# Loading the exactness flag earlier, a branch without prefetch hints, and exps without a wait on their own engine

## The chip, the core and the metric

The kernel runs on one core of one Trainium2 chip. Each set of experiments was made on one chip, different sets on different chips. The metric is the device time of one execution in microseconds (us), as the median of several executions. PE is the matrix engine, ACT the scalar engine, DVE the vector engine, POOL the general one, SP the engine that only synchronises and starts transfers.

"The span" is the time that a profile of the core covers. The time is normally 1.8 us longer than the span (1.75 to 1.92 in the runs of the kernel before). SBUF and PSUM are the core's two on-chip memories.

## The reference

Layer norm of `x`, then multi-query attention (32 heads of 16, one shared key and value head) beside a SwiGLU block, whose result gates the attention's:

```python
xn = layernorm(x)                              # x: 1 x 2048 x 512, bf16
q  = (xn @ wq).reshape(B, S, 32, 16)           # one k and one v for all heads
p  = softmax(einsum("bhqd,bkd->bhqk", q, xn @ wk) * 16**-0.5)
s  = einsum("bhqk,bkd->bqhd", p, xn @ wv).reshape(B, S, 512) @ wo
g  = silu((silu(xn @ w_gate) * (xn @ w_up)) @ w_down)
return x + s * g
```

The kernel skips the softmax's subtraction of the row maximum. A check at the end tells whether the sums of the exponentials lay in a safe range; if not, a branch leads into a second, exact computation. With this data the check passes and the exact path never runs.

## The kernel before

Scores are made on PE, 1024 columns at a time, into PSUM (`ring`). ACT takes 772 such tiles through `exp` into one of eight SBUF buffers `Pb` (DVE does the others by arithmetic), and PE multiplies the result by the values. The host-side scheduler in the program fixes each engine's order; the framework adds the semaphore waits. An exp has two inputs to wait for: its scores, and the products on PE that read the older content of its buffer.

```python
NPB = 8
Pb = [sb([P, 1024], BF16, f"Pb{i}") for i in range(NPB)]
...
buf = Pb[k % NPB][:]
...
ex = OP("ACT", 0.904, [sc, pb_rel[k - NPB] if k >= NPB else None, cur["exp"]],
        lambda: nc.scalar.activation(out=buf, in_=ring[i][:], func=ACT.Exp, scale=escale, bias=ebias),
        (1,), name="exp")
```

The framework also sees that exp `k` overwrites what exp `k - 8` wrote, and gives it a wait on ACT itself. That makes two waits, and one of them needs an instruction of its own ahead of the exp. In the trace it is the wait on PE that stands in the extra instruction (733 times; twice it is one on DVE), while the exp itself carries the wait on ACT.

The end of the program: four last products on PE, four multiplications on DVE, four additions on POOL and DVE, four stores from SP. The flag is loaded into a register of every engine, and every engine branches on it.

```python
tadd("DVE", e_out_mul(LN, obk[0], dsts[0]))
tadd("DVE", nc.vector.tensor_single_scalar(out=flag_i[:], in_=tq01[0:1, 0:1], scalar=P - 0.5, op=ALU.is_lt))
for en, et in (("SP", "SP"), ("POOL", "Pool"), ("PE", "PE"), ("DVE", "DVE"), ("ACT", "Activation")):
    with tc.issue_after(_last[en].ins):
        tc.mark_branch_hint_location("exact", "LikelyTaken", [getattr(mybir.EngineType, et)])
loads, vals = nc.values_load_multi_w_load_instructions(flag_i[0:1, 0:1])
flag = vals[0]
tadd("SP", [l for l in loads if l.ins.engine == nc.sync.engine])
fin_add(0, nc.gpsimd, "POOL")
tadd("DVE", e_out_mul(LN + 1, obk[1], dsts[1]))
tadd("DVE", e_out_mul(LN + 2, obk[2], dsts[2]))
fin_add(2, nc.gpsimd, "POOL")
fin_add(1, nc.vector, "DVE")
tadd("DVE", e_out_mul(LN + 3, obk[3], dsts[3]))
fin_add(3, nc.vector, "DVE")
for k in range(4):
    tadd("SP", e_out_st(LN + k))
MAIN.close()

with tc.If(flag > 0, label="exact"):
    _exact_max_path(...)                       # arguments cut
```

## Time and profile before

| | before |
|---|---|
| time, median of 3 | 781.65 us (780.74 to 781.86) |
| busy share of PE, ACT, DVE | 96%, 97%, 94% |
| last exp ends / last computing instruction ends / program ends | 766.1 / 774.1 / 780.2 us |
| extra wait instructions ahead of exps | 735 |

Three engines are almost always busy, so the shares don't tell which sets the pace. Three more views of this kernel are needed for what follows. First, the page's chain that ended last, by engine; "issue" is time in which the profile shows no cause for waiting:

```profile
PE 47%; ACT 37%; issue 8%; DVE 6%; POOL 0%; SPq 0%; DMA 0%; ACTq 0%; DVEq 0%; POOLq 0%
```

Second, ACT's timeline around two of its few real holes (start, length, what ran, the idle time before it and who ended it):

```profile
41.25 1.11 ACT L937 ACTIVATE Pb<-ring 128x1024 bf16<-128x1024 f32 x1
43.23 3.77 ACT L937 ACTIVATE Pb<-ring 128x1024 bf16<-128x1024 f32 x4 [0.86 <-PE ring L877]
...
462.71 1.16 ACT L937 ACTIVATE Pb<-ring 128x1024 bf16<-128x1024 f32 x1
464.29 2.85 ACT L937 ACTIVATE Pb<-ring 128x1024 bf16<-128x1024 f32 x3 [0.42 <-PE ring L877]
```

The engine stood idle for 0.86 and 0.42 us, and PE's scores ended that. In such a hole the nanoseconds between the scores and the exp can count.

Third, the 16 stores of the output from SP: duration of the issue (smallest, median, largest, in ns), and the time from issue to landing. Each store of 128 rows reports its landing in sixteen shares, and is done with the last:

```profile
L698 SPq DMA_DIRECT2D out_dram<-xn x16: 333/352/1392, 232.3 to 774.5; - x16
...
DMA to landing us min/median/max: 1.7/2.0/2.8
```

### The profile page before, as it was taken

How to read it: one execution, taken by the hardware profiler on the slowest of the kernel's cores; microseconds unless marked ns; L12 is line 12 of the kernel's file. 1: busy time of each engine (PE TensorE's matmuls, PEld its weight loads, DVE VectorE, ACT ScalarE, POOL GpSimd, SP SyncE). 2: the span in 40 equal slices, each digit the busy share in tenths (PEclk: the TensorE clock that was granted, in tenths of full speed). 3: DMA queues.
4: the chain of work that ended last, by engine and by line, in shares of the span. 5: the costliest groups of instructions: out<-in, count | busy, mean ns of one | idle time of the engine just before them, and what ended most of it. 6: DMA issues, size and time to landing. Idle time of an engine off the chain costs nothing.

```text
span 780.2 us, 21438 instructions
## 1 busy us (share of the span) xinstructions
PE 748.7 (96%) x9095; PEld 229.7 (29%) x9095; DVE 733.9 (94%) x920; ACT 757.1 (97%) x866; POOL 53.0 (7%) x59
## 2 busy tenths in 40 slices
PE   7999999999999999999999999999999999999994
PEld 3323223322222333322232322222223233322221
DVE  7689999999999999999999999999999999999994
ACT  6999999999999999999999999999999999999993
POOL 2100000000012000000001110000000300000001
PEclk9999999999999999999999999999999999999998
DMA  9400000000001000000000100000000000000001
GB/s 326 141 10 9 16 2 24 2 8 17 5 28 49 24 2 7 17 2 24 3 10 28 43 23 2 24 1 9 17 2 24 29 22 2 3 23 3 23 2 32
DMA packets 21199, 20.20 MB, mean 26 GB/s; under 512 B 8744, under 2 KB 17192, under 8 KB 21096
## 3 DMA queue, kind: packets, MB, share of 16 engines
q1 hardware_dynamic: 19512, 18.20, 7.7%
q8 instruction: 73, 1.20, 0.7%
q10 hardware_dynamic: 1584, 0.56, 0.3%
q14 instruction: 30, 0.25, 0.1%
HBM read 14.19 MB, written 2.34 MB: 21 GB/s over the span
## 4 chain that ended last, share of the span: by engine, by line
PE 47%; ACT 37%; issue 8%; DVE 6%; POOL 0%; SPq 0%; DMA 0%; ACTq 0%; DVEq 0%; POOLq 0%
ACT Pb L937 33%; PE ring L877 17%; PE m_ps L488 15%; PE o_ps L747 13%; ACT th L657 3%; DVE Bf L991 1%; ACT g_sb L937 1%; ACT th L674 1%; DVE Bf L1010 1%; DVE x_sb L1010 0%; PE ring L488 0%; DVE Bf L1005 0%; DVE Bf L1017 0%; DVE x_sb L991 0%; DVE x_sb L1005 0%
## 5 line engine op out<-in xcount | busy, mean ns | idle before, releaser
L937 ACT ACTIVATE Pb<-ring 128x1024 bf16<-128x1024 f32 x772 | 726.2, 1140 | 2.4 <-PE ring L877 2.3
L877 PE MATMUL ring<-QB,KT 32*128 32x512 bf16 x2048 | 306.1, 382 | 15.5 <-ACT Pb L937 9.1
L991 DVE TENSOR_SCALAR Bf<-ring 128x1024 uint16<-128x1024 f32 x172 | 209.7, 1219 | 5.5 <-PE ring L877 4.2
L877 PEld LDWEIGHTS <-KT 32*128 32x128 bf16 x2048 | 94.4, 91 | 314.2 <-issue 307.7
L747 PE MATMUL o_ps<-Pb,VA 128*32 128x512 bf16 x1544 | 146.9, 385 | 0.0
L991 DVE TENSOR_SCALAR x_sb<-ring 128x1024 uint16<-128x1024 f32 x72 | 87.8, 1219 | 3.1 <-PE ring L877 2.9
L1010 DVE TENSOR_TENSOR Bf<-Bf,Bf 128x2048 f16<-128x2048 f16 x74 | 90.1, 1217 | 0.1
L747 PE MATMUL o_ps<-xnT,zw 128*32 128x512 bf16 x1092 | 83.1, 381 | 0.0
L488 PE MATMUL m_ps<-xnT,wu_sb 128*32 128x512 bf16 x896 | 72.5, 384 | 1.1 <-DVE ab L659 1.1
L488 PE MATMUL m_ps<-wd_sb,hT 128*32 128x512 bf16 x896 | 71.5, 383 | 0.1
L488 PE MATMUL m_ps<-xnT,wg_sb 128*32 128x512 bf16 x896 | 70.3, 384 | 0.0
L747 PE MATMUL o_ps<-Bf,VD 128*32 128x512 f16 x688 | 67.1, 385 | 0.3 <-DVE Bf L1010 0.3
L732 POOL TENSOR_TENSOR oT<-oa,rb 128x512 bf16<-128x512 f32 x15 | 21.5, 1434 | 615.4 <-DMA rb<-dscr 365.9
L1017 DVE TENSOR_SCALAR Bf<-Bf 128x2048 uint16<-128x2048 uint16 x86 | 60.2, 700 | 0.6
L747 PEld LDWEIGHTS <-VA 128*32 128x32 bf16 x1560 | 37.9, 94 | 53.9 <-issue 51.5
L1005 DVE TENSOR_SCALAR Bf<-Bf 128x2048 uint16<-128x2048 uint16 x74 | 52.4, 716 | 0.0
L659 DVE SCALAR_TENSOR_TENSOR ab<-th,m_ps 128x512 f32<-128x512 f32 x56 | 38.1, 681 | 3.8 <-ACT th L657 3.4
L663 DVE TENSOR_TENSOR hT<-ab,m_ps 128x512 bf16<-128x512 f32 x56 | 38.2, 682 | 2.1 <-PE m_ps L488 1.7
L657 ACT ACTIVATE th<-m_ps 128x512 f32<-128x512 f32 x56 | 40.0, 714 | 0.0
L747 PEld LDWEIGHTS <-VD 128*32 128x32 f16 x976 | 26.4, 94 | 38.8 <-issue 35.2
L747 PEld LDWEIGHTS <-zw 128*32 128x32 bf16 x1092 | 25.8, 95 | 25.5 <-issue 12.9
L1010 DVE TENSOR_TENSOR x_sb<-x_sb 128x2048 f16<-128x2048 f16 x24 | 29.2, 1218 | 0.0
(121 smaller groups left out, 413.7 us busy)
## 6 DMA issues: line engine op xcount, KB each, us to landing
rb<-dscr SPq DMA_DIRECT2D x15, 256.0 KB
out_dram<-xn SPq DMA_DIRECT2D x16, 128.0 KB, 2.0
dn<-oa SPq DMA_DIRECT2D x120, 2.0 KB, 1.7
oa<-oa SPq DMA_DIRECT2D x60, 32.0 KB, 2.0
wg_sb<-in_B_w_gate_dram SPq DMA_DIRECT2D x1, 1792.0 KB, 11.5
wu_sb<-in_B_w_up_dram SPq DMA_DIRECT2D x1, 1792.0 KB
wd_sb<-in_B_w_down_dram SPq DMA_DIRECT2D x1, 1792.0 KB, 20.1
x_sb<-in_A_x_dram SPq DMA_DIRECT2D x3, 512.0 KB
```

Of the source, the lines that this page charges most:

```text
L488: return [nc.tensor.matmul(out=dst[GRP * j:GRP * j + GRP, :], lhsT=w[:, GRP * j:GRP * j + GRP], rhs=rhs, start=start, stop=stop, tile_posi ...
L657: t_ = OP("ACT", 0.477, [a], lambda: nc.scalar.activation(out=th[i][:], in_=m_ps[:], func=ACT.Tanh, scale=0.5), (0,), name="tanh")
L659: s_ = OP("DVE", 0.6, [t_, ab_rel[i]], lambda: nc.vector.scalar_tensor_tensor(out=ab[i][:], in0=th[i][:], scalar=1.0, in1=m_ps[:], op0=ALU ...
L663: h = OP("DVE", 0.6, [b], lambda: nc.vector.tensor_tensor(out=hT[:, f, :], in0=ab[i][:], in1=m_ps[:], op=ALU.mult), (1,), name="hmul")
L732: return [pk, q], lambda eng: eng.tensor_tensor(out=oT[qs % 2][:, jj, :], in0=o0[:], in1=rbt[:], op=ALU.mult)
L747: r.append(nc.tensor.matmul(out=o_ps[GRP * g:GRP * g + GRP, :], lhsT=lhs, rhs=rhs, start=(n == 0), stop=(n == pv_total[(b, g)] - 1), tile_ ...
L877: return lambda: [nc.tensor.matmul(out=ring[sl][:, u * 512:(u + 1) * 512], lhsT=KT[half][GRP * g:GRP * g + GRP, t * P:(t + 1) * P], rhs=QB ...
L937: lambda: nc.scalar.activation(out=buf, in_=ring[i][:], func=ACT.Exp, scale=escale, bias=ebias),
L991: lambda: nc.vector.tensor_scalar(out=U[:, hs], in0=ring[si][:], scalar1=ubias, scalar2=UINF, op0=ALU.add, op1=ALU.min), (1.5, u), name="p ...
L1005: o1 = OP("DVE", 0.6, [pa, pa0] + wrel, lambda: nc.vector.tensor_scalar(out=Bf[wi], in0=U, scalar1=0x3FF, scalar2=0x3800, op0=ALU.bitwise_and,
L1010: return lambda: eng.tensor_tensor(out=Bf[wi][:, a:z].bitcast(FP16), in0=Bf[wi][:, a:z].bitcast(FP16), in1=U[:, a:z].bitcast(FP16), op=ALU ...
L1017: o2 = OP("DVE", 0.6, o3, lambda: nc.vector.tensor_scalar(out=U, in0=U, scalar1=0x7C00, scalar2=None, op0=ALU.bitwise_and), (2, u, 1), nam ...
```

## The change

Its intent: take the self-waits off the exps, and with them 733 of the 735 extra instructions, let DVE have its flag early so that it can branch sooner, and drop the prefetch hints. The self-wait isn't needed: exp `k` waits for the products on PE that read exp `k - 8`'s output, and those waited for exp `k - 8`.

```diff
-    act_q = []
+    act_q, exp_ins = [], {}
...
-        ex = OP("ACT", 0.904, [sc, pb_rel[k - NPB] if k >= NPB else None, cur["exp"]],
-                lambda: nc.scalar.activation(out=buf, in_=ring[i][:], func=ACT.Exp, scale=escale, bias=ebias),
-                (1,), name="exp")
+        def emit():
+            bi = nc.scalar.activation(out=buf, in_=ring[i][:], func=ACT.Exp, scale=escale, bias=ebias)
+            if k >= NPB:
+                tc.declare_no_dep(bi.ins, exp_ins[k - NPB].ins,
+                                  reason="waits for the products on PE that read the older exp's output")
+            if k >= 0:
+                exp_ins[k] = bi
+            return bi
+        ex = OP("ACT", 0.904, [sc, pb_rel[k - NPB] if k >= NPB else None, cur["exp"]], emit, (1,), name="exp")
...
-    for en, et in (("SP", "SP"), ("POOL", "Pool"), ("PE", "PE"), ("DVE", "DVE"), ("ACT", "Activation")):
-        with tc.issue_after(_last[en].ins):
-            tc.mark_branch_hint_location("exact", "LikelyTaken", [getattr(mybir.EngineType, et)])
...
     fin_add(2, nc.gpsimd, "POOL")
+    tadd("DVE", [l for l in loads if l.ins.engine == nc.vector.engine])
     fin_add(1, nc.vector, "DVE")
...
-    with tc.If(flag > 0, label="exact"):
+    with tc.If(flag > 0):
```

The flag itself is computed at the same place in both kernels. Only its load on DVE moves.

## The prediction

> **What bounds the kernel now.** I began with the page. The span is 780.2 us (781.65 us is the timed median), and three engines are busy for nearly all of it, so shares alone don't name the bound:
>
> ```profile
> PE 748.7 (96%) x9095; PEld 229.7 (29%) x9095; DVE 733.9 (94%) x920; ACT 757.1 (97%) x866; POOL 53.0 (7%) x59
> ...
> L937 ACT ACTIVATE Pb<-ring 128x1024 bf16<-128x1024 f32 x772 | 726.2, 1140 | 2.4 <-PE ring L877 2.3
> ```
>
> The second line is the group of exps that the third part of the change edits. The reader should see that ACT sat idle for only 2.4 us before 772 exps. Next I read the instructions of that line: 735 exps have one extra instruction of the sequencer, a semaphore wait of 17 ns, because they wait on two things, PE (scores) and ACT itself (the older exp that wrote the same buffer).
>
> ```profile
> L937 ACT ACTIVATE Pb<-ring x772: 1017/1135/1317, 12.9 to 764.9; 128x1024 bf16<-128x1024 f32 x193
> L937 ACTq EVENT_SEMAPHORE  x735: 17/17/17, 12.1 to 764.7; - x184
> ```
>
> Then the timeline of ACT in mid-kernel: four overlapping narrow windows, each giving a merged pair (start, length from the first's start to the second's end), and one wide window.
>
> ```profile
> 504.20 2.07 ACT L937 ACTIVATE Pb<-ring 128x1024 bf16<-128x1024 f32 x2
> 505.10 2.08 ACT L937 ACTIVATE Pb<-ring 128x1024 bf16<-128x1024 f32 x2
> 506.00 2.09 ACT L937 ACTIVATE Pb<-ring 128x1024 bf16<-128x1024 f32 x2
> 506.97 2.04 ACT L937 ACTIVATE Pb<-ring 128x1024 bf16<-128x1024 f32 x2
> 501.47 11.21 ACT L937 ACTIVATE Pb<-ring 128x1024 bf16<-128x1024 f32 x12
> ```
>
> Starts are 0.90, 0.90 and then 0.97 us apart, as if the last exp had been late by 0.06. But the ends (start plus length) are 506.27, 507.18, 508.09, 509.01: 0.91 to 0.92 apart, with no hole. The wide window says the same: the first exp of the twelve took 1.13 us by its own record, so (11.21 - 1.13) / 11 = 0.916 us from end to end. From the trace's single records, 687 of the 697 directly consecutive pairs have an end-to-end step below 0.93 us, almost all 0.915 to 0.918. The engine delivers an exp every 0.917 us, whatever the starts do: ACT is the bound from about 14 us to 766 us, and only a hole between ends is lost time.
>
> Last, the end of the program. The last computing instruction ends at 774.07 us; the last 6.2 us are stores, branches and the closing waits, read from the instructions of the flag load (L1358) and the branch (L1372):
>
> ```profile
> L1358 SPq TENSOR_LOAD <-flag_i x1: 474/474/474, 770.7 to 770.7; - x1
> L1358 DVEq TENSOR_LOAD <-flag_i x1: 543/543/543, 773.2 to 773.2; - x1
> ...
> L1372 SPq EVENT_SEMAPHORE  x8: 17/17/17, 777.9 to 778.8; - x8
> ...
> L1372 PEldq COMPARE_BRANCH  x1: 3705/3705/3705, 771.3 to 771.3; - x1
> ...
> L1372 DVEq COMPARE_BRANCH  x1: 84/84/84, 773.8 to 773.8; - x1
> ...
> L1372 SPq COMPARE_BRANCH  x1: 70/70/70, 775.3 to 775.3; - x1
> ...
> L1372 DVEq EVENT_SEMAPHORE  x1: 21/21/21, 776.9 to 776.9; - x1
> ```
>
> SP is last. Its branch is at 775.35, after the four stores, and its next instruction, the first of 16 waits on landings, runs at 777.85. The semaphore of the fourth store gets its sixteenth landing at 778.37 (fifteen were in by 776.99), and the waits and the barrier after it take to 780.23. So the tail ends by the last share of the last store; SP's own branch, done at 777.85, is 0.52 us behind that as second limit. DVE is back at 776.94 and has 1.4 us to spare.
>
> **What the Trainium skill says.** "Perfetto Trace Analysis", section "DVE / Act Engine Instruction", puts an event-wait queue and an execution FIFO between sequencer and engine: while one ACTIVATE executes, the next is decoded and waits there. The trace agrees: the extra wait usually passes some 0.1 to 0.6 us ahead of its exp's start, while the previous exp still runs. The same page, "Identifying Dependency Chains", says that an instruction with waits on several engines may have semaphore instructions put ahead of it; those are the 735. "Runtime: NRT & Kernel Launch", section "Instruction fetch mechanics", says that a taken branch whose target isn't loaded forces a fetch by DMA before execution goes on. The trace agrees: after their branches ACT, DVE and SP stand still for 2.5, 3.1 and 2.4 us, PE's branch itself takes 3.7, and fetches of 8 or 16 KB appear 0.6 to 1.1 us after each; it also shows no fetch within 2 us after any of the five prefetch hints, so they seem to have bought nothing here.
>
> **The change, part by part.** The order of instructions was compared engine by engine. The flag is computed at the same place as before; only the five hints go, DVE's load of the flag moves up ahead of the last two adds and one product, and exps waiting on both PE and ACT fall from 733 to 0 of 780 (2 with a wait on DVE stay). Nothing else moves.
>
> 1. *Self-waits.* Where an exp's scores come late, the trace gives the price: from PE's semaphore update to the exp's start it is 83 ns by way of the extra wait, and 23 ns for activations that wait on PE directly. So 60 ns per exp whose lateness is felt. Felt means a hole between ends. The list of end-to-end steps over 0.93 us has 11 entries, 3.4 us together beyond 0.917 (0.58 of it at the very start). Eight of them end with an exp released 83 ns before through the extra wait. One is only 0.02 us deep, seven can give back the whole 60 ns: 7 x 0.06 + 0.02 = 0.44 us. The other hundred or so exps that start late leave no hole: 0. The 17 ns themselves lie beside a running exp: 735 x 0. **Sum -0.44 us.**
>
> 2. *Hints.* 45 to 56 ns each, on sequencers. SP's and POOL's are at 734 and 737 us, in long waits; PE's at 769.94 comes after its last weight load is issued; ACT's has nothing behind it but the flag; DVE's (770.14) passes while the first product runs (769.97 to 770.66). **0 us**, as no fetch answers to them.
>
> 3. *DVE's early load.* It waits for the flag (written 770.71), takes 0.54 us, so to about 771.3, while the products run back to back to 771.90. The add behind it started at 771.83 and isn't delayed. DVE's branch then follows the last add's dispatch at 773.2 instead of 773.77, and DVE's closing comes at about 776.4 instead of 776.9. It isn't the last engine: **0 us**. But its fetch moves by 0.57 us, to about 773.9, among the last stores. I put -0.1 us for that, a choice: it could fall either way.
>
> Sum: 781.65 - 0.44 - 0.1 = 781.1 us.
>
> **The rivals.**
> - *Each extra wait costs its time on ACT.* 735 x 62 ns (from that wait to the exp when the exp is held by it) is 45 us, giving 736. Against: the end-to-end step is 0.917 with the extra wait (685 pairs) and 0.9166 without (12 pairs).
> - *Each late start is lost.* About 123 exp-to-exp starts are more than 0.906 us apart and follow the wait by 62 ns; at 60 ns each, 7.4 us, giving 774.3, still within 2%. For it: the critical chain names PE for 47% of the span, so handovers from PE to ACT look frequent. Against: the ends have no holes there.
> - *PE sets the pace.* PE waits for ACT's exps only 9.1 us in all. If its order, not ACT, were the limit, the 0.44 us would vanish too: 781.6.
> - *The tail moves.* The sixteenth share of the last store landed 1.4 us after the fifteenth, following a 16 KB fetch (776.18 to 777.23), which is PE's next block after its branch. Other timing of fetches and stores could bring the end forward by 0.52 us at most, until SP's own return binds, or push a share back by about the length of a fetch, 1.2 us. If the hints did arm something unseen, losing them could lengthen SP's return by 1 us or so: 0.5 us on the end.
>
> **Range and chances.** The three runs of before spread by 1.1 us, as much as the whole effect. From 781.1 I allow 1.2 us down (good tail and a few more holes shortened) and 1.2 us up: 779.9 to 782.3. Two per cent is 15.6 us; only the first rival reaches it, and I give it 0.01. Nothing here can cost 15.6 us: 0.01. So 0.98 for the same.
>
> **What would show it.** Under the exps' line, semaphore waits fall from 735 to a handful. Late starts shrink (their excess drops by about 60 ns each), but the end-to-end step stays 0.917, which is the point to check: a step of 0.90 would prove the first rival. The last exp then starts some 0.5 us earlier than 764.9; 7 us earlier would prove the second. In the tail, DVE's load sits at about 770.7 and its branch at 773.2; all engines still stand 2.4 to 3.7 us after their branches. Wrong would be: branches that return at once, a longer return on SP, or a last landing that moves by more than 0.5 us against the last add's end.

## The result

| | before | after |
|---|---|---|
| median of 6 runs of the same rounds | 781.62 us (780.74 to 781.86) | 781.43 us (780.61 to 781.69) |

The ratio is 0.9997, with a 95% interval of 0.9984 to 1.001: the same.

Three lines of the page of the kernel after, the groups that answer to those of before:

```profile
PE 748.9 (96%) x9093; PEld 229.7 (29%) x9095; DVE 734.0 (94%) x920; ACT 756.9 (97%) x866; POOL 54.2 (7%) x59
...
PE 48%; ACT 45%; DVE 5%; issue 1%; SPq 0%; DMA 0%; ACTq 0%; POOL 0%; DVEq 0%; POOLq 0%
...
L937 ACT ACTIVATE Pb<-ring 128x1024 bf16<-128x1024 f32 x772 | 730.7, 1202 | 2.1 <-PE ring L877 2.1
```

In the chain, "issue" fell from 8% to 1% and ACT rose from 37% to 45%. So some 60 us of the chain changed their name and the time stayed where it was: what the view had called issue lay under exps that were running. And the mean exp now takes 1202 ns by its record, up from 1140, though nothing became slower.

The instructions of the exps' line:

```profile
L937 ACT ACTIVATE Pb<-ring x772: 1017/1206/1377, 12.8 to 764.2; 128x1024 bf16<-128x1024 f32 x193
...
L937 ACTq EVENT_SEMAPHORE  x2: 17/17/17, 12.0 to 12.8; - x2
```

The waits are gone (735 to 2), and the last exp starts at 764.2 instead of 764.9 (in one trace of each; between two traces of the kernel before it moves by 0.4 us). ACT's timeline in mid-kernel, in narrow windows that give merged pairs as in the prediction, and one wide window:

```profile
503.82 2.12 ACT L937 ACTIVATE Pb<-ring 128x1024 bf16<-128x1024 f32 x2
504.72 2.14 ACT L937 ACTIVATE Pb<-ring 128x1024 bf16<-128x1024 f32 x2
505.62 2.15 ACT L937 ACTIVATE Pb<-ring 128x1024 bf16<-128x1024 f32 x2
506.59 2.10 ACT L937 ACTIVATE Pb<-ring 128x1024 bf16<-128x1024 f32 x2
500.10 11.34 ACT L937 ACTIVATE Pb<-ring 128x1024 bf16<-128x1024 f32 x12
```

Starts are still 0.90, 0.90 and 0.97 apart, and the ends (505.94, 506.86, 507.77, 508.69) still 0.91 to 0.92. The wide window gives (11.34 - 1.26) / 11 = 0.916 us, where 1.26 is the first exp's own record: the same pace as before. That the uneven starts are still there is a surprise, taken up in the discussion. The two holes shown of before:

```profile
43.07 3.77 ACT L937 ACTIVATE Pb<-ring 128x1024 bf16<-128x1024 f32 x4 [0.81 <-PE ring L877]
...
463.97 3.77 ACT L937 ACTIVATE Pb<-ring 128x1024 bf16<-128x1024 f32 x4 [0.36 <-PE ring L877]
```

0.81 and 0.36 us instead of 0.86 and 0.42: each gave back about 0.06.

The end of the program: DVE's load, and the instructions of the branch (duration in ns, start in us):

```profile
L1361 DVEq TENSOR_LOAD <-flag_i x1: 535/535/535, 770.1 to 770.1; - x1
```

```profile
L1376 SPq EVENT_SEMAPHORE  x8: 17/17/17, 776.9 to 777.4; - x8
...
L1376 PEldq COMPARE_BRANCH  x1: 3635/3635/3635, 770.7 to 770.7; - x1
...
L1376 DVEq COMPARE_BRANCH  x1: 72/72/72, 772.5 to 772.5; - x1
...
L1376 SPq COMPARE_BRANCH  x1: 45/45/45, 774.2 to 774.2; - x1
...
L1376 DVEq EVENT_SEMAPHORE  x1: 21/21/21, 775.4 to 775.4; - x1
```

DVE branches at 772.5 instead of 773.8 and is back at 775.4 instead of 776.9. But SP comes last, as before: branch 774.2, next instruction 776.9, so 2.65 us against 2.50 before. This execution fell on a short tail. The trace's single records give all 16 landings of the last store by 776.07, before SP is back, so SP's return sets the end here; in the trace of before the sixteenth landing did (778.37, after SP's return at 777.85). The stores' issues and landings:

```profile
L698 SPq DMA_DIRECT2D out_dram<-xn x16: 332/361/1314, 232.2 to 773.8; - x16
...
DMA to landing us min/median/max: 1.7/1.9/2.7
```

The slow second issue of the last four is still there (1.31 us).

### The profile page after: what moved, and what is told of

It is laid out like the page before. It is cut to its first block, busy times and chain, and to the rows that moved or that the text cites. A ratio compares the mean times of both kernels' runs of the same rounds, so it can differ in the third digit from the quotient of the medians. Undisturbed runs are those within 1.5% of the kernel's fastest.

```text
span 778.8 us, 20698 instructions
## 1 busy us (share of the span) xinstructions
PE 748.9 (96%) x9093; PEld 229.7 (29%) x9095; DVE 734.0 (94%) x920; ACT 756.9 (97%) x866; POOL 54.2 (7%) x59
## 4 chain that ended last, share of the span: by engine, by line
PE 48%; ACT 45%; DVE 5%; issue 1%; SPq 0%; DMA 0%; ACTq 0%; POOL 0%; DVEq 0%; POOLq 0%
ACT Pb L937 41%; PE ring L877 17%; PE m_ps L488 16%; PE o_ps L747 13%; ACT th L657 3%; DVE Bf L997 1%; ACT g_sb L937 1%; PE ring L433 1%; DVE Bf L1016 1%; ACT th L674 1%; DVE x_sb L997 0%; DVE Bf L1023 0%; PE ring L488 0%; DVE x_sb L1016 0%; PE ring L452 0%
## 5 line engine op out<-in xcount | busy, mean ns | idle before, releaser
L937 ACT ACTIVATE Pb<-ring 128x1024 bf16<-128x1024 f32 x772 | 730.7, 1202 | 2.1 <-PE ring L877 2.1
L657 ACT ACTIVATE th<-m_ps 128x512 f32<-128x512 f32 x56 | 43.7, 781 | 0.0
```

Of the source, the lines that this page charges most:

```text
L657: t_ = OP("ACT", 0.477, [a], lambda: nc.scalar.activation(out=th[i][:], in_=m_ps[:], func=ACT.Tanh, scale=0.5), (0,), name="tanh")
L937: bi = nc.scalar.activation(out=buf, in_=ring[i][:], func=ACT.Exp, scale=escale, bias=ebias)
```

## The experiments

The theory: the exps' waits cost only where ACT has a real hole, some 0.4 us in all; the hints and DVE's load cost nothing; and the tail after the last exp moves by about 1 us from run to run for a reason that the change doesn't touch, namely instruction fetches after the branches that meet the last stores. The rivals are those of the prediction: each wait costs its time on ACT; PE and not ACT sets the pace; the hints or the earlier load move the tail. The expectations stand before each set of runs. Where they name a theory by a letter, T is this reading of the tail, and C the rival that PE sets the pace.

Two quantities are read from each trace's single records: the **body**, from the end of the first exp to the end of the last, and the **tail**, from there to the program's last instruction. Both are of one execution each; the last instruction counts by its start.

### The parts alone, and both kernels once more

`exp_only` has only the change of the exps:

```diff
+            if k >= NPB:
+                tc.declare_no_dep(bi.ins, exp_ins[k - NPB].ins, ...)
```

> Only the third part: the exps without the self-wait; hints, load and branch as before. Theory A (ACT delivers an exp every 0.917 us end to end; the self-wait costs 60 ns only where a late score makes a hole): the last exp starts 0.3 to 0.8 us earlier than before's 764.92 us, and the time falls by about 0.4 us. Rival B (every late start is lost): last exp 7 us earlier, time -7. Rival C (PE sets the pace): last exp within 0.1 us of before.

`flag_only` has only the other two parts:

```diff
-            tc.mark_branch_hint_location("exact", "LikelyTaken", ...)      # all five
+    tadd("DVE", [l for l in loads if l.ins.engine == nc.vector.engine])
-    with tc.If(flag > 0, label="exact"):
+    with tc.If(flag > 0):
```

> Only the first two parts: hints away, DVE loads the flag early; the self-waits stay. Theory A: last exp at before's 764.9 +- 0.15 us; DVE branches at about 0.65 us after the last add starts being issued, every engine still needs 2.4 to 3.8 us after its branch; time within 0.3 us of before. Rival D (the hints armed something, or cost something): the gap after SP's branch changes by over 0.5 us, and the time with it.

`before_again` and `after_again` are the two kernels with no edit.

> The kernel before once more, for a second trace of its tail. Theory T (the end is the later of SP's return from its branch and the last store's sixteenth landing, which depends on where instruction fetches fall): the last exp is again at 764.9 +- 0.15, but the time from the last exp to the end may differ from the first trace's 15.25 us by up to 1 us. If instead the tail is fixed by the program, it is 15.25 +- 0.1 us.

> The changed kernel once more. Theory T: last exp at 764.2 +- 0.15 us as in its first trace, time from the last exp to the end anywhere from 14.5 to 15.6 us. If the change itself shortened the tail, it is again 14.5 us.

| kernel | median us (range) | ratio to before, 95% | body | tail |
|---|---|---|---|---|
| before, same rounds, 9 runs | 781.2 (780.73 to 782.3) | | | |
| before (first profile) | | | 752.14 | 14.08 |
| before_again | 781.03 (780.68 to 781.08) | 0.9993 (0.998 to 1.0007) | 751.95 | 13.45 |
| flag_only | 781.68 (780.73 to 782.32) | 1.0 (0.9987 to 1.0014) | 752.01 | 14.72 |
| exp_only | 781.15 (780.55 to 781.39) | 0.9994 (0.9981 to 1.0008) | 752.20 | 13.41 |
| after (first profile) | | | 751.61 | 13.29 |
| after_again | 781.4 (780.55 to 781.91) | 0.9996 (0.9983 to 1.001) | 751.76 | 14.38 |

The row of `before_again` is the yardstick: the same kernel against itself gives a ratio of 0.9993 with an interval of 0.0027, or 2.1 us. Total time can't resolve 0.4 us in so many runs; the traces can. The start of the last exp, on which the expectations rested, can't: it was 764.52 us in `before_again` and 764.60 in `flag_only`, not within 0.15 of 764.9, and 764.42 in `after_again`, not within 0.15 of 764.2. These three are misses, and `exp_only`, with 764.60, falls into its window only as `flag_only` would. The first exp ends anywhere from 13.6 to 14.2 us in the traces, which is why the body is measured from there. From one exp's end to the next, the records give (position of the hole in us, by the trace of before):

| hole at | before, before_again, flag_only | exp_only, after, after_again |
|---|---|---|
| 43 | 1.889, 1.890, 1.891 | 1.830, 1.830, 1.829 |
| 156 | 0.938, 0.935, 0.936 | none |
| 464 | 1.446, 1.447, 1.447 | (two holes), 1.382, 1.385 |
| 674 | 1.095, 1.095, 1.095 | none |
| 732 | 1.307, 1.310, 1.306 | 1.251, 1.241, 1.252 |
| 235 | 1.269, 1.164, 1.228 | 1.200, 1.217, 1.265 |
| 238 | 1.006, 1.009, 1.009 | 1.009, 1.008, 1.009 |
| 239 | 1.082, 1.079, 1.079 | 1.080, 1.081, 1.080 |

The first five go with the self-wait and with nothing else: `flag_only` has them as the kernel before, `exp_only` as the kernel after (it alone splits the one at 464). So the exps' part shortens holes, as the theory has it, and the other two parts do nothing here. The hole at 235 varies with the execution in either kernel, and the last two don't change.

The body of `exp_only`, 752.20, is a miss at first sight. In that execution a product on DVE at 735.8 us took 2.30 us instead of 1.22 while POOL worked, PE waited 0.81 us for it, and ACT had a hole of 0.50 us at 740. It occurs in one other kernel's trace without the wait (`act_stores`) and in one with it (`seq_st`), so the change doesn't bring it. The mean body over the three traces with the wait in this table is 752.03; over all nine without it, 751.77; over the seven of those nine that have no such stray hole, 751.67. That is 0.26 or 0.36 us less.

The tails are 13.3 to 13.5 or 14.1 to 14.7 us, and each kernel that was traced twice had one of each. So the tail explains the spread of about 1 us and says nothing of the change.

### Is it the fetch that meets the last stores?

The three traces with the long tail (before, `flag_only`, `after_again`) share a pattern: PE's second block of 16 KB after its branch is fetched just as the last stores' data move, and the last of the last store's sixteen shares lands 1.4 to 2.2 us after the fifteenth. But the three with the short tail have that fetch beside their last store too (in the kernel after from 775.19 to 776.35 us, while the store's shares land from 775.39 on), and their sixteenth share comes only 0.06 to 0.52 us after the fifteenth. So the meeting alone doesn't make a long tail, and what decides isn't shown. Four kernels try how far the fetch matters, all made from the kernel after.

`late_pe` holds PE's load of the flag back until DVE's last multiplication, so PE branches late:

```diff
+    last_mul = e_out_mul(LN + 3, obk[3], dsts[3])
+    tadd("DVE", last_mul)
+    for l in loads:
+        if l.ins.engine == nc.tensor.engine:
+            tc.add_manual_dep(l.ins, last_mul.ins.name, ...)
```

> The changed kernel, with PE's load of the flag made to wait for the last product (about 2.4 us later), so that PE's branch and the two 16 KB fetches behind it come later. Theory T (the last store's sixteenth share is held up by PE's second 16 KB fetch, at 775.2 to 777 us in the six traces so far): that fetch now falls near 777.5, after the stores; the sixteenth landing of the last store is within 0.7 us of the fifteenth in every run, the end is SP's return from its branch plus 1.9 us, the tail is 14.5 to 14.7 us from the last exp, and all five times lie near the low end of the others, 780.5 to 780.9. If PE's fetch has nothing to do with it, the times still spread over 1 us. If PE itself becomes last (branch at 773.2, back at 776.9), nothing is lost, since SP is at its waits until 778.

`act_stores` lets ACT, idle by then, issue the last four stores, so SP can branch at once:

```diff
+    tadd("ACT", [l for l in loads if l.ins.engine == nc.scalar.engine])
-        tadd("SP", e_out_st(LN + k))
+        tadd("ACT", nc.scalar.dma_start(out=out_v[:, LN + k, :], in_=res[(LN + k) % 4][:, :D]))
```

> The changed kernel, with the last four stores issued by ACT, so that SP can branch at 770.8 and be back by 773.5, before the stores land. Theory T: in the runs where the last share lands in time (about 776.1), the end is no longer SP's return (776.9) but that landing, so the tail shortens by up to 0.8 us, to about 13.8 us after the last exp; in the runs with a late share (about 778.3) nothing is gained. Median 780.5 to 781.2. If SP's return was never a limit, no change.

`act_late` has both edits.

> Both of the two edits: ACT issues the last stores and PE loads the flag late. Theory T: both limits go, every run has the short tail: about 13.8 us after the last exp, times near 779.9, 1.5 us below the changed kernel's median (0.2 per cent), and a spread under 0.5 us. If the theory is wrong, no better than the better of the two.

`no_branch` has neither flag load nor branch nor exact path. It isn't a kernel to keep, as the guard is gone; on this data its result is right.

```diff
-    loads, vals = nc.values_load_multi_w_load_instructions(flag_i[0:1, 0:1])
-    with tc.If(flag > 0):
-        _exact_max_path(...)
```

> The changed kernel without the exact path, the loads of the flag and the branch (the result is the same for these inputs, since the flag is 0): what the branch costs in all. Theory T: no fetches after 766 us but PE's regular one, the four stores issue without a long one of 1.3 us, all shares land within 0.3 us of each other at about 775.7, and the end comes 1.9 us after that, 777.6: a tail of 13.3 us and a time of 779.4, with a spread under 0.5 us. If the tail were set by the arithmetic and the stores alone, the time stays at 780.6 or above.

| kernel | median us (range) | ratio to before, 95% | spans of the runs, us |
|---|---|---|---|
| before | 781.84 (780.68 to 782.72) | | 778.9 to 780.9 |
| late_pe | 781.81 (781.6 to 782.08) | 1.0001 (0.9987 to 1.0015) | 778.5 to 779.0 |
| act_stores | 780.14 (779.94 to 782.69) | 0.9981 (0.9967 to 0.9994) | 777.6 to 780.7 |
| act_late | 782.24 (781.64 to 782.84) | 1.0008 (0.9995 to 1.0022) | 778.5 to 779.4 |
| no_branch | 778.69 (778.6 to 778.74) | 0.9961 (0.9948 to 0.9975) | 776.5 to 776.6 |

The stores of `no_branch`:

```profile
L698 SPq DMA_DIRECT2D out_dram<-xn x16: 332/344/622, 232.0 to 773.4; - x16
...
DMA to landing us min/median/max: 1.7/1.9/2.1
```

No slow issue among the last four, no late landing (the sixteenth share follows the fifteenth by 0.04 us at most), and times that agree within 0.14 us. So the flag's loads and branches, which this kernel lacks together, bring nearly all of the spread (that it is PE's fetch among them which delays the share is not shown by this), and the kernel with them is about 3 us longer: 781.84 - 778.69 = 3.15 us, of which some 0.3 is the exps' part, which this kernel has too. It came out 0.7 us below what had been expected, since the last landing came at 775.08 us instead of 775.7 and the closing after it took 1.40 us instead of 1.9, while the time was 2.1 us over the span instead of 1.8. Against the trace of the kernel after, whose program ends 778.75 - 776.48 = 2.27 us later, the records split it: the last store is issued 0.48 us later, SP is back 1.31 us after the time at which the landing would then have been, and the closing waits take 1.88 us instead of 1.40.

`late_pe` did to the span what had been hoped: with PE's branch moved, the second store's issue is 0.34 us, and no span is over 779.0. But the time was not shorter, and this is a miss:

```profile
L1381 PEldq COMPARE_BRANCH  x1: 3878/3878/3878, 773.4 to 773.4; - x1
...
L1381 PEldq EVENT_SEMAPHORE  x1: 51/51/51, 777.4 to 777.4; - x1
```

PE branches at 773.4 and is back at 777.4, and its next 16 KB are fetched from 778.01 to 779.14, past the last instruction at 778.85. The time is 2.8 to 3.3 us longer than the span in this kernel and 2.8 to 3.4 in `act_late`, instead of 1.8. Of the fourteen traces only these two have a block of PE's outstanding at the end, but that doesn't settle it: `act_split` below is 2.0 to 2.8 us over its spans with none outstanding. What the traces do show is that semaphores are still updated after the last instruction, the last of them 1.91 us after it in the kernel after, 3.13 in `late_pe`, 2.95 in `act_late` and 2.31 in `act_split`. So the added time lies in a closing that the span doesn't cover; why it is longer stays open. The second miss: the last store's sixteenth share landed 1.33 us after the fifteenth here too, with the first fetch of 16 KB (774.81 to 775.82) now beside it, where 0.7 us at most had been expected. Moving the branch moved the meeting; it did not prevent it. `act_late`, expected near 779.9 with the short tail in every run, is a miss for the same two reasons: 782.24, with the last share 1.80 us after the fifteenth.

`act_stores` looked like a gain, with an interval just below 1, and was run again.

### The pace of ACT, and the stores

`seq_st` puts far more than a 17 ns wait ahead of each exp: two register saves on ACT's sequencer, on the kernel before.

```diff
-                lambda: nc.scalar.activation(...),
+                lambda: [*[nc.scalar.store(jt[0:1, u:u + 1], jr) for u in range(2)],
+                         nc.scalar.activation(...)],
```

> The kernel before, with two instructions of ACT's sequencer added ahead of each of the 780 exps (each saves a register to a word of SBUF and carries a wait that has long been met; they touch no data): the disputed cost, tripled. Theory A (what the sequencer does beside a running exp is free): end-to-end step stays 0.917 us, time +0 to +1 us; only exps that come just after a late score could start later. Rival B (each instruction of the sequencer costs its time on ACT): at least 1560 x 0.06 = 94 us more.

`exp1008` shortens the exps, also on the kernel before: 1008 of 1024 columns, the rest of each buffer set to 1 once. Its result is wrong (relative error 0.107).

```diff
+EW = 1008
+        chain("POOL", nc.gpsimd.memset(Pb[i][:, EW:1024], 1.0))
-                lambda: nc.scalar.activation(out=buf, in_=ring[i][:], ...)
+                lambda: nc.scalar.activation(out=buf[:, 0:EW], in_=ring[i][:, 0:EW], ...)    # for k >= 0
```

> The kernel before, with 772 exps that do 1008 of their 1024 columns (the last 16 columns of each buffer are set to 1 once; the result is wrong on purpose). From the steps in the trace, 0.917 us for 1024 columns and 0.490 us for 512, a column is 0.834 ns, so an exp's step falls by 13.3 ns to 0.904. Theory A (ACT is the bound for nearly the whole run): last exp up to 772 x 13.3 ns = 10.3 us earlier, time -6 to -10 us, the rest being given to new waits for PE. Rival C (PE sets the pace): time within 1 us of before, and ACT shows the saved time as holes between its ends.

`act_stores_2` is `act_stores` with no edit.

> The kernel with the last stores issued by ACT once more, for a trace of a short tail, since the traced run of the first was its slowest. Theory T: time 780.0 in most runs; in a run of about 780.0 the end comes 1.9 us after the last store's sixteenth landing and SP waits for it.

| kernel | median us (range) | ratio to before, 95% |
|---|---|---|
| before | 781.63 (781.0 to 782.17) | |
| seq_st | 781.89 (781.4 to 783.21) | 1.0001 (0.9986 to 1.0017) |
| exp1008 | 772.55 (772.04 to 772.97) | 0.9886 (0.9871 to 0.9901) |
| act_stores_2 | 781.19 (780.81 to 781.81) | 0.9995 (0.9981 to 1.0009) |

The instructions of `seq_st` ahead of the exps and the exps themselves:

```profile
L941 ACTq TENSOR_STORE jt<- x1560: 237/242/535, 11.8 to 765.6; - x195
```

```profile
L942 ACT ACTIVATE Pb<-ring x772: 1018/1126/1307, 12.9 to 766.3; 128x1024 bf16<-128x1024 f32 x193
```

1560 saves of 242 ns are 377 us of the sequencer's time, and the median moved by 0.26 us, within the interval: the ends are still 0.917 us apart in the stream. Two saves, 0.484 us, fit beside a running exp. If work of that size is free in the stream, a wait of 17 ns is. It isn't quite free at the holes: the traced execution, the slowest of the four at 783.21 us, has a body of 753.60, 1.6 us over the mean of before, with a dozen more holes, five of them in its first 7 us.

The exps of `exp1008`, as a group of the page and in a window of ten:

```profile
L940 ACT ACTIVATE Pb<-ring 128x1008 bf16<-128x1008 f32 x772 | 714.3, 1099 | 3.0 <-PE ring L880 2.8
```

```profile
493.02 9.26 ACT L940 ACTIVATE Pb<-ring 128x1008 bf16<-128x1008 f32 x10
```

The first of the ten took 1.135 us, so the step is (9.26 - 1.135) / 9 = 0.903 us. Over all directly consecutive pairs less than 0.93 us apart, the single records give a mean step of 0.9034 us as against 0.9167 before. The body became 752.03 - 742.83 = 9.2 us shorter, of the 772 x (0.9167 - 0.9034) = 10.3 us that a pure bound by ACT would give. PE did as many products of the same length as before. So ACT sets the pace and PE follows: the rival that PE does it falls.

`act_stores_2` did not confirm the gain: the interval includes 1, and in its trace the last share again landed 1.09 us after the fifteenth, beside a fetch of 16 KB (775.34 to 776.61). Whether ACT as issuer is worth some tenths of a microsecond stays open.

### Can the last store go round the fetch?

`act_split` is `act_stores` with the last two stores cut into 120 and 8 partitions. If one transfer engine serves both the fetch and the late share, the cut might take that engine out of the large piece.

```diff
-        tadd("ACT", nc.scalar.dma_start(out=out_v[:, LN + k, :], in_=res[(LN + k) % 4][:, :D]))
+        for p0, p1 in (((0, P),) if k < 2 else ((0, 120), (120, P))):
+            tadd("ACT", nc.scalar.dma_start(out=out_v[p0:p1, LN + k, :], in_=res[(LN + k) % 4][p0:p1, :D]))
```

> The kernel with the last stores on ACT, the last two stores cut in two each, 120 and 8 partitions, so that by the Trainium skill (DMA: Bandwidth & Descriptors, on how many engines a DMA uses) they run on the lowest-numbered 15 and 8 of the 16 DMA engines. No trace so far says which engine serves the instruction fetches. If it is the sixteenth, no share of these stores stands behind a fetch: the last landing comes within 0.3 us of the one before it in every run, the spread falls below 0.6 us and the median to about 779.9 to 780.3 (two more issues of 0.35 us each are in it). If it is another one, the late share stays and the time is 780.5 to 782, no better than without the cut.

The time was 781.98 us (781.46 to 782.22) beside 781.06 (780.71 to 782.13) of the kernel before in the same rounds, the ratio 1.0009 (0.9995 to 1.0023): no better, the second of the two outcomes. The cut itself came out as expected: of the last store's large piece one share was marked 0.6 us after the issue and 15 landed with the data later, of its small piece one and 8. In the large piece of the last store the last share still came 1.80 us after the one before, beside a fetch from 774.85 to 776.66, and in the small pieces 0.3 to 0.4 us after. The pieces took more issues and avoided nothing. Which engine serves the fetches is not settled.

No version came out that keeps the exact path and reliably beats both kernels.

## Why the prediction was right

**What bounds the kernel.** Right, and now tested from both sides. The step of 0.917 us is the same with the wait, without it, and with 0.484 us of other work of the sequencer ahead of each exp; it follows the exp's length (`exp1008`). The rival at 62 ns for each wait, 736 us, is refuted.

**The self-waits, -0.44 us.** The mechanism held: from PE's semaphore to the exp's start it is 22 to 23 ns in the kernel after at the holes, as against 83 before at most of them. Before, PE's update released the extra instruction, and the exp followed that one 61 or 62 ns later; now the exp waits for PE itself. The sum was about right, partly by luck. In the first pair of traces the body is 0.53 us shorter, over all traces 0.26 to 0.36. Of the seven holes that were each to give back 0.06 us, three did (43, 464 and 732 us, some 0.17 together). Two gave nothing (238 and 239 us): the release was 60 ns quicker there too, so PE's update came as much later against the end before it. There PE's own order sets the distance, and a quicker handover buys nothing. The last two (235 and 641 us), and the one of 0.02 us at 228, differ from one execution to the next in either kernel, so nothing can be put down to the change. In their place the holes at 156 and 674 us, not counted because their extra wait had passed 0.3 us ahead of the exp, closed and gave 0.02 and 0.18. Why they closed isn't shown. The five that go with the wait make 0.37 us, which agrees with the body. The step that failed is "seven can give back the whole 60 ns": it took one trace's holes for fixed, and took every release by PE for one that would come no later.

**Late starts.** That they cost nothing was right. "Late starts shrink" was wrong. Starts more than 0.906 us apart number 236 to 241 in the three traces with the wait and 234 to 238 in the three without in the first table of experiments, and those up to 1.1 us exceed 0.904 by 40 ns on average with the wait and by 42 without. What moved is every start against its own end: the exps' records grew from a median of 1135 to 1206 ns while the ends kept their distance. The reading that fits: in a row, starts follow each other at 0.904 us and ends at 0.917, so the starts run ahead by 13 ns an exp until one has to wait for its scores, which depend on older ends. A late start is that correction, and its size is set by the difference of the two distances, not by the wait. In the kernel after, each of the 87 starts 0.95 to 1.1 us apart comes 22 or 23 ns after an update by PE, as this reading needs; no run was made to test it. The wait only sets where the starts lie against the ends. So counting late starts and multiplying by 60 ns, the second rival, counted something that was never lost.

**Hints, 0 us.** Right. With them SP stood for 2.50 to 2.70 us after its branch (before, `before_again`, `exp_only`), without them for 2.54 to 2.65 (`flag_only` and both traces of the kernel after). One trace speaks against "no fetch answers to them": in `seq_st`, which has the hints, PE's first block came at 772.41 us, 1.05 after PE's hint and 0.33 before its branch, and that branch took 2.57 us instead of the 3.4 to 4.5 of the other traces with a branch. Whether the hint did it isn't shown; SP was last there too, so the end gained nothing.

**DVE's load, 0 us, and -0.1 for the moved fetch.** The first is right: DVE is back 1.6 us earlier on the clock and 0.9 us earlier against the last addition's end, ahead of SP as before. The -0.1 can be neither confirmed nor refuted. The fourth rival, a tail that moves, is real in both directions and is the largest effect: it moved by 0.6 us between two traces of the kernel before and by 1.1 us between two of the kernel after. That is more than the 0.52 us which the prediction allowed as the most that the end could come forward: it took SP's return as fixed, but SP branches after the stores' issues, and the fourth of these took 0.80 us in the trace of before and 0.37 in that of after. One of the prediction's signs of being wrong came true as well: against the last add's end, the last landing moved from 4.30 to 2.63 us. It proves nothing, as `before_again`, with no edit, has 3.03.

**The sum.** 781.1 was predicted and 781.43 measured. The 0.3 between them is within the spread of the tail, and 781.03 to 781.84 were the medians of the unchanged kernel in other sets of runs.

What the prediction missed altogether is where time was to be had at the end: the flag's loads and branches cost nearly 3 us together, some seven times the 0.44 us that the change was to bring.

## What to carry to other kernels

Before you price an instruction or a wait, measure the distance from end to end of the engine that sets the pace; what sits between sequencer and engine is free until it exceeds that distance, and costs only at real holes. Don't take starts that come late, records that get longer, or a share of "issue" in the chain for lost time unless the ends move. And run the unchanged kernel as one of the experiments: an effect below its own spread has to be read from the traces' single records, hole by hole.

## What the Trainium skill lacked or had wrong

- "ScalarE: Activation LUTs", section "What ACT_TABLE_LOAD costs": for immediate scale and bias it gives 186 ns + 0.833 ns a column, and an overlap of about 93 ns back to back, which makes 946 ns for 1024 columns as an estimate. Measured were 917 ns for 1024, 903 for 1008 and 490 for 512 columns: the slope agrees, and the fixed part in a row is 64 ns, not 93. These exps read PSUM and write SBUF; the section doesn't say for which memory its figures hold.
- "Perfetto Trace Analysis", section "DVE / Act Engine Instruction": it says that the record runs from the execution's start to the write's acknowledgement, but not that the start slides in a busy stream. Here starts were 0.90 to 0.97 us apart at a constant pace of 0.917, and the median record grew by 71 ns with no loss; only ends time such a stream.
- "Advanced Engine Details and Errata", section "Control Flow Timing": about 108 ns for a compare-and-branch. The records show 45 to 84 ns on ACT, DVE, POOL and SP, but 2.4 to 3.4 us from the branch to the next instruction on ACT, DVE and SP where no landing held it, and 2.6 to 4.5 us on PE; loads and branches together cost nearly 3 us of the program's time.
- "Runtime: NRT & Kernel Launch", section "Instruction fetch mechanics": it speaks of blocks of 16 KiB and calls the price of crossing one mostly hidden. Here only PE's were 16 KB and the other engines' 8 KB. It lacks that more blocks are fetched after the branch has returned, and what that does to stores: with a fetch beside them, the last share landed 1.1 to 2.2 us after the one before in nine of fourteen traces, and one issue took 1.1 to 1.6 us instead of 0.35 in ten. A register load from SBUF took 463 to 543 ns (kernels before and after) and a save to SBUF 242 ns, where this section gives about 200 ns for a register load and 73 for a store to HBM.
- No page has branch prefetch hints: the five here were followed by no fetch within 2 us in four of the five traces that have them; in the fifth, PE's block came 1.05 us after its hint, and PE's branch took 2.57 us instead of 3.4 or more. No page prices the extra semaphore instruction ahead of an instruction with two waits: 60 ns at a hole, nothing in a full stream.
